# Windowed attention with global rows, then a softplus MLP: global rows through DRAM, a four-slot attention period, and a prologue issued from three queues

## The chip, the core and the metric

The kernel runs on one core of one Trainium2 chip. The metric is the device time of one execution in microseconds (us). The core's engines run side by side, each through its own instruction queue in program order: TensorE (PE in the profile) multiplies matrices into PSUM, VectorE (DVE), ScalarE (ACT) and GpSimd (POOL) work element by element, and SyncE (SP) issues transfers. Transfers can be issued from SP, ACT and POOL; sixteen DMA engines carry them out. Engines wait for one another through semaphores.

## The reference

Eight batches, eight heads, 576 positions, 64 elements per head. Each position attends to the positions within 32 of it and to eight global positions, which are given at run time by `global_idx`; a global position attends to all. The result, as 4608 tokens of 512, goes through a two-layer MLP with softplus.

```python
scores = scale * np.matmul(q, k.transpose(0, 1, 3, 2))
mask = np.abs(pos[:, None] - pos[None, :]) <= window
mask = mask | is_global[:, None] | is_global[None, :]
attn = softmax(np.where(mask, scores, -1e9)); attn_out = np.matmul(attn, v)
x = attn_out.transpose(0, 2, 1, 3).reshape(4608, 512)
h = x @ w_in                                    # 512 -> 2048
out = log(1 + exp(h)) @ w_out                   # 2048 -> 512
```

## The kernel before

**Attention.** A batch is cut into five token tiles (`NTL`), four of 120 positions and one of 96. Behind the positions of each tile stand the eight global rows, so that a tile of 128 (or 104) keys holds its own window and the global keys. The heads are worked on in four pairs `p` (`NP`). Per pair:

- `transposes` (L230) turns five token tiles of K on TensorE into one PSUM tile (`tp`, one buffer) and VectorE copies them to `KT` in two copies (L235, L237); the same again for Q.
- `scores(p, grp)` (L241) multiplies K tiles by the queries in their window: three tiles in group 0 and two in group 1, for both heads. The PSUM tile `sc` has one buffer. ScalarE takes the exponential (L251) and VectorE multiplies by the mask (L252).
- `values(b, h)` (L258), once for each head of the pair, multiplies V (with a block of ones beside it, so that the sums come out as well) by the masked exponentials, into the PSUM tile `av` (one buffer, two banks). VectorE copies sums and values out to `uz` (L278, L279).
- `normalise` (L283) adds up the global rows' parts (L288, L290), makes 1/sum as exp(-ln(sum)) on ScalarE (L292, L293), and GpSimd multiplies (L296, L298) into `xT`, the transposed MLP input.

When a batch's four pairs are done, `globals_out` (L300) writes the eight global rows into their places in `xT` with eight GpSimd copies at positions known at run time (L306).

**Global rows.** SP and POOL read the eight positions into registers (L73). K's and Q's rows of all batches are gathered to `kgf` and `qgf` with eight transfers each (L129), converted and transposed on TensorE once (L216 to L222), and for every batch GpSimd's `glob_cols` (L225 to L228) copies them into the last columns of each tile of `KT` and `QT`. V's rows are gathered into `vg_f` (L134) and put behind each V tile by a small transfer of its own (L111).

**Loading.** Every K, Q and V tile of float32 goes through one ring of six buffers (`ld`, L91). SP issues the load (L93), GpSimd converts to bfloat16 (L98, L115), and a seventh load waits until the oldest conversion is done.

**MLP.** Nine tiles `n` of 512 tokens (`n_tiles`). `mm1(n, s)` (L311) makes 128 hidden rows with four matmuls into `h` (two buffers), and ScalarE makes the softplus from an exponential (L319) and a logarithm (L320). `mm2(n, s)` (L324) does four of the sixteen matmuls of an output block (PSUM tile `o`, one buffer); after the fourth VectorE copies it out (L334) and SP stores it (L335).

**The order.** It is written by hand (`manual_schedule`): what an engine does, and in which sequence, is the order of the calls. First comes a prologue: loads of batch 0, gathers, constants, masks (L138 to L210), the attention of batch 0, and the first slots of batch 1. Then each tile `n` has sixteen slots `s`; a slot calls `mm1(n, s)`, the attention pieces of this slot, and `mm2(n-1, s)`. `attention_slots(b)` (L338) gives batch `b` its slots, counted from the start of tile `b-1`: loads and conversions at -9 to -2, and pair `p` at 3p-3 (transposes), 3p-2 and 3p-1 (scores), 3p+1 and 3p+2 (values), 3p+3 (`normalise`). Tile `n` needs batch `n`, so batch `b` runs beside tile `b-1`; tiles 7 and 8 have no attention beside them.

Of the kernel before, what the change touches and what calls it, by code (L numbers as in the profile page):

```python
# [11 lines left out]
FP32 = mybir.dt.float32  # L12
# [25 lines left out]
def kernel(  # L38
# [22 lines left out]
    nc.scalar.preload_act_table_set("natural_log_exp_and_others")  # L61

# [5 lines left out]
    gidx_i = global_idx.rearrange("(one n) -> one n", one=1).bitcast(I32)  # L68
    idx_i = const.tile([P, 2 * NG], I32)
    nc.sync.dma_start(out=idx_i[:], in_=gidx_i.to_broadcast([P, 2 * NG]))  # L70

    engines = [mybir.EngineType.SP, mybir.EngineType.Pool]
    regs = [  # L73
        nc.values_load(idx_i[0:1, 2 * g:2 * g + 1], engines=engines, min_val=0, max_val=S - 1,
                       skip_runtime_bounds_check_because="positions of the sequence")
        for g in range(NG)
    ]


# [6 lines left out]
    ident = const.tile([P, P], FP32)  # L86
    ident_bf = const.tile([P, P], BF16)


    def load(src, b, t, tag):  # L90
        f = work.tile([P, H, D], FP32, tag="ld", bufs=6, name=f"{tag}_f")  # L91
        s0 = KW * t
        nc.sync.dma_start(out=f[:ST[t]], in_=src[b, :, s0:s0 + ST[t], :].rearrange("h s d -> s h d"))  # L93
        return f

    def load_cast(src, b, t, dst, tag):
        f = load(src, b, t, tag)
        nc.gpsimd.tensor_copy(dst[:ST[t], t], f[:ST[t]].rearrange("p h d -> p (h d)"))  # L98

    def load_k(b):  # L100
        kb = work.tile([P, NTL, d_model], BF16, tag="kb", bufs=1)
        return kb, [lambda t=t: load_cast(k, b, t, kb, "k") for t in range(NTL)]

    def load_q(b):
        qb = work.tile([P, NTL, d_model], BF16, tag="qb", bufs=1)
        return qb, [lambda t=t: load_cast(q, b, t, qb, "q") for t in range(NTL)]

    def load_v_tile(b, t):
        f = load(v, b, t, "v")
        n = ST[t]  # L110
        nc.sync.dma_start(out=f[n:n + NG], in_=vg_f[:, b])  # L111
        dst = V1[b % 2][:, t]
        vf = f[:n + NG].rearrange("p (a e) d -> p a e d", e=2)
        o = dst[:n + NG].rearrange("p a (c d) -> p a c d", d=D)
        nc.gpsimd.tensor_copy(o[:, :, 0:3:2, :], vf)  # L115


    kb0, ks = load_k(0)
    qb0, qs = load_q(0)
    for f in ks:  # L120
        f()

    vg_f = const.tile([NG, B, H, D], FP32)
    kg_f = work.tile([B * NP, NG, 2 * D], FP32, tag="gt", bufs=2, name="kgf")
    qg_f = work.tile([B * NP, NG, 2 * D], FP32, tag="gt", bufs=2, name="qgf")
    for src, dst in ((k, kg_f), (q, qg_f)):
        sv = src.rearrange("b (a e) s d -> (b a) e s d", e=2)
        for g in range(NG):
            nc.sync.dma_start(out=dst[:, g:g + 1, :].rearrange("p o (e d) -> p e o d", e=2),  # L129
                              in_=sv[:, :, bass.ds(regs[g], 1), :])  # L130
    for f in qs:
        f()
    for g in range(NG):
        nc.sync.dma_start(out=vg_f[g:g + 1].rearrange("o b h d -> o (b h) d"),  # L134
                          in_=v.rearrange("b h s d -> (b h) s d")[:, bass.ds(regs[g], 1), :].rearrange("c o d -> o c d"))


    make_identity(nc, ident[:])  # L138
    nc.vector.tensor_copy(ident_bf[:], ident[:])
    for i in range(2):  # L140
        nc.vector.memset(V1[i][:], 0.0)
        nc.vector.memset(V1[i][:, :, :, D:2 * D], 1.0)
    nc.vector.memset(KT[:, :, 4, :], 0.0)
    nc.vector.memset(QT[:, :, 4, :], 0.0)

    idx_f = const.tile([P, NG], FP32)
    nc.vector.tensor_copy(idx_f[:], idx_i[:].rearrange("p (n two) -> p n two", two=2)[:, :, 0])

# [4 lines left out]
    same = work.tile([P, NG, NG], FP32, tag="m1")  # L153
    nc.vector.tensor_tensor(out=same[:], in0=idx_f[:].unsqueeze(2).to_broadcast([P, NG, NG]),
                            in1=idx_f[:].unsqueeze(1).to_broadcast([P, NG, NG]), op=ALU.is_equal)
    nc.vector.tensor_tensor(out=same[:], in0=same[:], in1=low[:], op=ALU.mult)
    uq = work.tile([P, NG], FP32, tag="m2")
    nc.vector.tensor_reduce(out=uq[:], in_=same[:], axis=AX.X, op=ALU.max)
    nc.vector.tensor_scalar(out=uq[:], in0=uq[:], scalar1=-1.0, scalar2=1.0, op0=ALU.mult, op1=ALU.add)
# [3 lines left out]
    kidx = work.tile([P, NTL], FP32, tag="m4")  # L163
    nc.vector.tensor_copy(kidx[:], kidx_i[:])
    keq = work.tile([P, NTL, NG], FP32, tag="m5")
    nc.vector.tensor_tensor(out=keq[:], in0=kidx[:].unsqueeze(2).to_broadcast([P, NTL, NG]),
                            in1=idx_f[:].unsqueeze(1).to_broadcast([P, NTL, NG]), op=ALU.is_equal)
    akey = const.tile([P, NTL], FP32)
    nc.vector.tensor_reduce(out=akey[:], in_=keq[:], axis=AX.X, op=ALU.max)
    nc.vector.tensor_scalar(out=akey[:], in0=akey[:], scalar1=-1.0, scalar2=1.0, op0=ALU.mult, op1=ALU.add)  # L170
    vld = const.tile([P, NTL], FP32)
    nc.gpsimd.memset(vld[:], 1.0)
    ukey = const.tile([P, 2], FP32)
    for i, (s, c) in enumerate(((KW, slice(0, 4)), (ST[4], slice(4, 5)))):
        nc.gpsimd.affine_select(out=vld[:, c], in_=vld[:, c], compare_op=ALU.is_ge, fill=0.0, base=s - 1,
                                channel_multiplier=-1, pattern=[[0, c.stop - c.start]])
        dg = work.tile([P, NG], FP32, tag=f"m6{i}")
        nc.gpsimd.memset(dg[:], 1.0)
        nc.gpsimd.affine_select(out=dg[:], in_=dg[:], compare_op=ALU.is_equal, fill=0.0, base=-s,
                                channel_multiplier=1, pattern=[[-1, NG]])  # L180
        nc.vector.tensor_tensor(out=dg[:], in0=dg[:], in1=uq[:], op=ALU.mult)
        nc.vector.tensor_reduce(out=ukey[:, i:i + 1], in_=dg[:], axis=AX.X, op=ALU.max)
    nc.vector.tensor_tensor(out=akey[:], in0=akey[:], in1=vld[:], op=ALU.mult)
# [11 lines left out]
                            channel_multiplier=1, pattern=[[-1, 32]])  # L195
    masks = [const.tile([P, GW[i]], BF16, name=f"mask{i}") for i in range(2)]
# [16 lines left out]
    gT = []  # L213
    for f in (kg_f, qg_f):
        gb = work.tile([B * NP, NG, 2 * D], BF16, tag="ex0", bufs=2, name="gb")
        nc.vector.tensor_copy(gb[:], f[:])  # L216
        ps = psum.tile([P, NG, B * NP], BF16, tag="tp")
        for g in range(NG):
            nc.tensor.transpose(out=ps[:, g, :], in_=gb[:, g, :], identity=ident_bf[:B * NP, :B * NP])  # L219
        t_ = const.tile([P, B * NP, NG], BF16, name=f"gT{len(gT)}")  # L220
        nc.vector.tensor_copy(t_[:].rearrange("p c g -> p g c"), ps[:])
        gT.append(t_)  # L222


    def glob_cols(b, dst, src):  # L225
        s = src[:, b * NP:(b + 1) * NP, :]
        nc.gpsimd.tensor_copy(dst[:, :, 0:4, KW:KW + NG], s.unsqueeze(2).to_broadcast([P, NP, 4, NG]))  # L227
        nc.gpsimd.tensor_copy(dst[:, :, 4, ST[4]:ST[4] + NG], s)  # L228

    def transposes(src, dst, p):  # L230
        ps = psum.tile([P, NTL * P], BF16, tag="tp", name="tp")
        for t in range(NTL):
            nc.tensor.transpose(out=ps[:, t * P:t * P + ST[t]], in_=src[:ST[t], t, p * P:(p + 1) * P],  # L233
                                identity=ident_bf[:ST[t], :ST[t]])
        nc.vector.tensor_copy(dst[:, p, 0:4, 0:KW],  # L235
                              ps[:, 0:512].rearrange("p (t c) -> p t c", c=P)[:, :, 0:KW])
        nc.vector.tensor_copy(dst[:, p, 4, 0:ST[4]], ps[:, 512:512 + ST[4]])  # L237
# [3 lines left out]
    def scores(p, grp):  # L241
# [9 lines left out]
        nc.scalar.activation(out=ex[:], in_=sc[:, :, 0:GW[grp]], func=ACTF.Exp, scale=SCALE)  # L251
        nc.vector.tensor_tensor(out=ex[:], in0=ex[:], in1=masks[grp][:].unsqueeze(1).to_broadcast([P, 2, GW[grp]]),  # L252
                                op=ALU.mult)
        exps[p, grp] = ex

    UZ = {}

    def values(b, h):  # L258
        p, e = h // 2, h % 2
        av = psum.tile([P, 1024], FP32, tag="av")  # L260
        off = 512 - SPLIT
        parts = []
        for t in range(NTL):
            cuts = [WLO[t]] + ([SPLIT] if WLO[t] < SPLIT < WHI[t] else []) + [WHI[t]]
            for lo, hi in zip(cuts, cuts[1:]):
                parts.append((t, lo, hi))
        for i, (t, lo, hi) in enumerate(parts):
            grp = 0 if t in GRP[0] else 1
            ex = exps[p, grp]
            c = GOFF[t] + lo - WLO[t]  # L270
            nc.tensor.matmul(out=av[:, off + lo:off + hi], lhsT=V1[b % 2][:, t, p, 64 * e:64 * e + 128],  # L271
                             rhs=ex[:, e, c:c + hi - lo],
# [63 lines left out]


    def attention_slots(b):  # L338
        kq = {}

        def loads_kq(which, fs):
            for f in fs:
                f()
# [121 lines left out]
```

## Time and profile before

| | before |
|---|---|
| median of three runs | 505.02 us (504.61 to 507.24) |
| profiled execution, own time | 505.82 us |
| its span, first to last instruction | 504.1 us |
| busy: TensorE, ScalarE, VectorE, GpSimd | 350.6, 272.0, 232.5, 152.9 us |
| transferred by the DMA queues | 43.41 MB |
| mean granted TensorE clock | 0.972 |

Busy times don't add up to the span, since the engines overlap, and a busy TensorE isn't one at full speed: its matmuls are pipelined, and the profile's duration of one includes the pipeline. Spacing between starts is the better measure. In rows of the order of time the columns are start, duration, engine, line, operation, what is written `<-` what is read, the number of instructions merged into the row, and in brackets the idle time before it and what ended it. In rows by group stand the number of instructions, busy time, mean in ns, and idle time of the engine ahead of them.

### The profile page before, as it was taken

What the parts mean: (1) busy time and instruction counts of PE and PEld (TensorE: products, weight loads), DVE (VectorE), ACT (ScalarE), POOL (GpSimd) and SP (SyncE); (2) the same over time, 40 slices, a digit from 0 to 9 for tenths busy, and PEclk for the clock granted to TensorE, in tenths of its full rate; (3) what the DMA queues carried; (4) which work ended last, traced back from release to release, by engine and by line L of the source; (5) the groups of instructions that cost most, each with busy time, mean ns of one, the idle gap of its engine ahead of it and who ended that gap; (6) DMA issues with size and microseconds to landing.
All of it is one profiled execution on the core that took longest, in us unless ns stands there. A gap on an engine that the chain in (4) does not pass through costs nothing.

```text
span 504.1 us, 6355 instructions
## 1 busy us (share of the span) xinstructions
PE 350.6 (70%) x2192; PEld 170.3 (34%) x2192; DVE 232.5 (46%) x479; ACT 272.0 (54%) x417; POOL 152.9 (30%) x310
## 2 busy tenths in 40 slices
PE   0000343102786997799699869968996999999985
PEld 0000222001432443354245425424542544444432
DVE  0028455501584684286358628735862774001111
ACT  1000232201687786488468757856874787766720
POOL 1142311444137135513722461263256113000000
PEclk9999999999987999899899999989998999999999
DMA  5369730099535039425902963391296100111111
GB/s 77 53 114 184 121 58 0 0 169 202 84 59 113 2 82 199 93 61 92 198 23 62 169 127 79 76 198 38 62 169 123 42 22 26 37 42 44 42 43 62
DMA packets 124561, 43.41 MB, mean 86 GB/s; under 512 B 115505, under 2 KB 119601, under 8 KB 124529
## 3 DMA queue, kind: packets, MB, share of 16 engines
q1 hardware_dynamic: 120304, 38.82, 40.9%
q0 software_dynamic: 4224, 4.19, 5.2%
q8 instruction: 17, 0.28, 0.2%
q14 instruction: 16, 0.12, 0.1%
HBM read 37.10 MB, written 9.44 MB: 92 GB/s over the span
## 4 chain that ended last, share of the span: by engine, by line
PE 45%; DMA 18%; ACT 10%; DVE 9%; SPq 6%; issue 6%; POOL 5%; POOLq 0%; DVEq 0%
PE o L330 19%; PE hp L316 17%; DMA v_f<-vg_f 7%; DMA k_f<-in_k_dram 6%; DMA q_f<-in_q_dram 5%; ACT ex L251 4%; PE av L271 4%; PE sc L247 3%; SPq L93 3%; DVE ot L334 2%; ACT e L319 2%; PE tp L233 2%; SPq L129 2%; DVE uz L279 2%; ACT gt L320 2%
## 5 line engine op out<-in xcount | busy, mean ns | idle before, releaser
L330 PE MATMUL o<-w_out_t,gt 128*128 128x512 bf16 x576 | 148.7, 384 | 13.9 <-DVE ot L334 13.9
L316 PE MATMUL hp<-xT,w_in_t 128*128 128x512 bf16 x576 | 155.9, 395 | 0.0
L319 ACT ACTIVATE e<-hp 128x512 f32<-128x512 f32 x144 | 85.6, 595 | 87.5 <-PE hp L316 86.4
L251 ACT ACTIVATE ex<-sc 128x1008 bf16<-128x1008 f32 x64 | 58.3, 912 | 101.0 <-PE sc L247 101.0
L320 ACT ACTIVATE gt<-e 128x512 bf16<-128x512 f32 x144 | 90.9, 632 | 4.6
L296 POOL TENSOR_TENSOR xT<-uz,rz 128x480 bf16<-128x480 f32 x32 | 38.4, 1201 | 174.2 <-ACT rz L293 174.2
L316 PEld LDWEIGHTS <-w_in_t 128*128 128x128 bf16 x576 | 55.8, 101 | 65.3 <-issue 9.3
L330 PEld LDWEIGHTS <-gt 128*128 128x128 bf16 x576 | 51.8, 98 | 73.7 <-issue 24.6
L278 DVE COPY uz<-av 64x616 f32<-64x616 f32 x64 | 51.0, 797 | 37.5 <-PE av L271 36.5
L334 DVE COPY ot<-o 128x512 f32<-128x512 f32 x36 | 24.8, 690 | 71.1 <-PE o L330 70.5
L279 DVE COPY uz<-av 64x616 f32<-64x616 f32 x64 | 51.0, 797 | 1.4
L247 PE MATMUL sc<-QT,KT 64*128 64x200 bf16 (+2 forms) x320 | 26.8, 268 | 23.4 <-POOL QT L227 15.8
L233 PE MATMUL tp<-ident_bf,kb 120*128 120x120 bf16 (+1 forms) x160 | 17.2, 230 | 35.8 <-POOL kb L98 34.4
L252 DVE TENSOR_TENSOR ex<-ex,mask_223 128x1008 bf16<-128x1008 bf16 x32 | 22.2, 693 | 40.4 <-ACT ex L251 39.5
L98 POOL CAST kb<-k_f 120x512 bf16<-120x512 f32 (+1 forms) x40 | 24.6, 615 | 48.7 <-DMA k_f<-in_k_dram 48.7
L219 PE MATMUL ps<-ident_bf,gb 32*128 32x32 bf16 x16 | 0.8, 185 | 51.2 <-DVE gb L216 51.2
L98 POOL CAST qb<-q_f 120x512 bf16<-120x512 f32 (+1 forms) x40 | 27.1, 678 | 26.1 <-DMA q_f<-in_q_dram 26.1
L235 DVE COPY KT<-tp 128x480 bf16<-128x480 bf16 x32 | 13.0, 406 | 40.2 <-PE tp L233 40.0
L292 ACT ACTIVATE rz<-uz 128x616 f32<-128x616 f32 x32 | 22.5, 704 | 16.2 <-DVE uz L278 16.2
L271 PE MATMUL av<-ex,V_0_106 128*128 128x160 bf16 (+2 forms) x192 | 20.8, 253 | 10.5 <-DVE uz L279 10.4
L233 PEld LDWEIGHTS <-kb 120*128 120x128 bf16 (+1 forms) x160 | 12.8, 105 | 45.3 <-POOL kb L98 36.9
L252 DVE TENSOR_TENSOR ex<-ex,mask_224 128x800 bf16<-128x800 bf16 x32 | 18.4, 576 | 20.5 <-ACT ex L251 19.9
(76 smaller groups left out, 245.4 us busy)
## 6 DMA issues: line engine op xcount, KB each, us to landing
out_dram<-ot SPq DMA_DIRECT2D x36, 256.0 KB
k_f<-in_k_dram SPq DMA_DIRECT2D x32, 240.0 KB
q_f<-in_q_dram SPq DMA_DIRECT2D x32, 240.0 KB
v_f<-in_v_dram SPq DMA_DIRECT2D x32, 240.0 KB
w_in_t<-in_moe_w_in_dram POOLq DMA_DIRECT2D x4, 512.0 KB, 8.1
w_out_t<-in_moe_w_out_dram POOLq DMA_DIRECT2D x4, 512.0 KB, 9.6
k_f<-in_k_dram SPq DMA_DIRECT2D x8, 192.0 KB
q_f<-in_q_dram SPq DMA_DIRECT2D x8, 192.0 KB
```

The costliest lines, as they stand in the source:

```text
L98: nc.gpsimd.tensor_copy(dst[:ST[t], t], f[:ST[t]].rearrange("p h d -> p (h d)"))
L233: nc.tensor.transpose(out=ps[:, t * P:t * P + ST[t]], in_=src[:ST[t], t, p * P:(p + 1) * P], identity=ident_bf[:ST[t], :ST[t]])
L247: nc.tensor.matmul(out=sc[:, e, GOFF[t]:GOFF[t] + w], lhsT=KT[r, p, t, :], rhs=QT[r, p].rearrange("p t c -> p (t c)")[:, WLO[t]:WHI[t]], s ...
L251: nc.scalar.activation(out=ex[:], in_=sc[:, :, 0:GW[grp]], func=ACTF.Exp, scale=SCALE)
L252: nc.vector.tensor_tensor(out=ex[:], in0=ex[:], in1=masks[grp][:].unsqueeze(1).to_broadcast([P, 2, GW[grp]]), op=ALU.mult)
L271: nc.tensor.matmul(out=av[:, off + lo:off + hi], lhsT=V1[b % 2][:, t, p, 64 * e:64 * e + 128], rhs=ex[:, e, c:c + hi - lo], start=(lo in ( ...
L278: nc.vector.tensor_copy(UZ[p][ur, 1, :], av[zr, off:off + NPOS])
L279: nc.vector.tensor_copy(UZ[p][ur, 0, :], av[ur, off:off + NPOS])
L316: nc.tensor.matmul(out=hp[:], lhsT=w_in_t[:, kd, kf * P:(kf + 1) * P], rhs=xT[:, kd, n * NT:(n + 1) * NT], start=(kd == 0), stop=(kd == KD ...
L319: nc.scalar.activation(out=e[:], in_=hp[:], func=ACTF.Exp)
L320: nc.scalar.activation(out=gts[n][:, kf, :], in_=e[:], func=ACTF.Ln, bias=1.0)
L330: nc.tensor.matmul(out=op[:], lhsT=gts[n][:, kf, i * P:(i + 1) * P], rhs=w_out_t[:, kf, :], start=(kf == 0), stop=(kf == KF - 1))
```

## The change

**Global rows.** Three DRAM buffers hold the eight rows of all batches for K, Q and V. Each is gathered once, with eight transfers; K's and V's are issued from ScalarE, Q's from GpSimd, and the positions are read into registers of those two. For each batch and tensor two transfers on SP then put the rows behind the five token tiles in a float32 tile that holds the whole batch. There is one such tile each for K, Q and V, in place of the ring. A conversion takes all 128 partitions of a token tile, rows included, and so K and Q are transposed together with their global rows, 128 columns a tile, and copied out with one copy. The separate transposing of the rows, `glob_cols` and the zeroing of `KT`, `QT` and V's tiles are gone; the unused partitions of the last tile are zeroed in the float32 tile.

**Period.** Pair `p` starts at slot 4p-6 and is spread over the two halves of the slots: half 0 stands between `mm1` and `mm2`, half 1 behind `mm2`. Loads are issued at slots -18 (K), -15 (Q) and -11 (V), conversions stand at -9 to -4. `normalise` is split into the sums of the global rows, logarithm, exponential and scaling, at slots of their own.

**Prologue.** SP issues the loads of K and Q of batch 0 first, then V, then the rows; the index is loaded from ScalarE. VectorE converts K and GpSimd converts Q and V of batch 0. In batch 0's attention ScalarE copies Q's transposes and the sums, Q's transposes use a buffer of `h`, and the value products stand between the other pieces. The loads of `w_out` move into the first four slots of tile 0.

```diff
+    stage = {n: const.tile([P, NTL, d_model], FP32, name=f"{n}_f") for n in "kqv"}
+    grow = {n: nc.dram_tensor(f"{n}_global_rows", (NG, B * H * D), FP32, kind="Internal").ap() for n in "kqv"}
+    def load(n, b, eng=None):
+        eng = eng or nc.sync
+        for t in range(NTL):
+            s0 = KW * t
+            eng.dma_start(out=stage[n][:ST[t], t].rearrange("p (h d) -> p h d", d=D),
+                          in_=src[n][b, :, s0:s0 + ST[t], :].rearrange("h s d -> s h d"))
+    def load_rows(n, b, eng=None):
+        eng = eng or nc.sync
+        g = grow[n][:, b * H * D:(b + 1) * H * D]
+        eng.dma_start(out=stage[n][KW:P, 0:4], in_=g.unsqueeze(1).to_broadcast([NG, 4, H * D]))
+        eng.dma_start(out=stage[n][ST[4]:ST[4] + NG, 4], in_=g)
+    def gather(n, eng, regs):
+        sv = src[n].rearrange("b h s d -> (b h) s d")
         for g in range(NG):
+            eng.dma_start(out=grow[n][g:g + 1].rearrange("o (c d) -> c o d", d=D),
+                          in_=sv[:, bass.ds(regs[g], 1), :])
+    def cast_tile(n, b, t, eng):
+        if n == "v":
+            o = V1[b % 2][:, t].rearrange("p a (c d) -> p a c d", d=D)[:, :, 0:3:2, :]
+            eng.tensor_copy(o, stage[n][:, t].rearrange("p (a e d) -> p a e d", e=2, d=D))
+            return
+        if t == 0:
+            kqb[n] = work.tile([P, NTL, d_model], BF16, tag=f"{n}b", bufs=1, name=f"{n}b")
+        eng.tensor_copy(kqb[n][:, t], stage[n][:, t])
...
+    for n in "kqv":
+        nc.gpsimd.memset(stage[n][96:P, 4], 0.0)
+    load("k", 0)
+    load("q", 0)
...
+    gather("k", nc.scalar, regs)
+    gather("q", nc.gpsimd, regs)
+    gather("v", nc.scalar, regs)
+    load("v", 0)
+    for n in "kqv":
+        load_rows(n, 0)
...
-    def glob_cols(b, dst, src):
...
+    def transposes(n, p, tag="tp", copy=None):
+        dst = KT if n == "k" else QT
+        ps = psum.tile([P, 2 * 512], BF16, tag=tag, bufs=2 if tag == "h" else 1, name="tp")
         for t in range(NTL):
+            nc.tensor.transpose(out=ps[:, t * P:(t + 1) * P], in_=kqb[n][:, t, p * P:(p + 1) * P],
+                                identity=ident_bf[:])
+        (copy or nc.vector.tensor_copy)(dst[:, p].rearrange("p t c -> p (t c)"), ps[:, 0:NTL * P])
...
-        nc.vector.tensor_copy(UZ[p][ur, 1, :], av[zr, off:off + NPOS])
+        (zcopy or nc.vector.tensor_copy)(UZ[p][ur, 1, :], av[zr, off:off + NPOS])
...
+        at(-18, 1, load, "k", b)
+        at(-18, 1, load_rows, "k", b)
+        at(-15, 1, load, "q", b)
+        at(-15, 1, load_rows, "q", b)
+        at(-11, 1, load, "v", b)
+        at(-11, 1, load_rows, "v", b)
         for t in range(NTL):
+            at(-9 + t // 3, 0, cast_tile, "k", b, t, nc.gpsimd)
+            at(-8 + t // 3, 1, cast_tile, "q", b, t, nc.gpsimd)
+            at(-6 + t // 2, 1, cast_tile, "v", b, t, nc.gpsimd)
         for p in range(NP):
+            s = 4 * p - 6
+            at(s, 0, transposes, "k", p)
+            at(s, 1, transposes, "q", p)
+            at(s + 1, 0, scores, p, 0)
+            at(s + 1, 1, mask, p, 0)
+            at(s + 2, 0, scores, p, 1)
+            at(s + 2, 1, mask, p, 1)
+            at(s + 3, 0, values, b, p, 0)
+            at(s + 4, 1, values, b, p, 1)
+            at(s + 5, 1, glob_sums, b, p)
+            late = 1 if p < NP - 1 else 0
+            at(s + 6 + late, 0, inv_ln, p)
+            at(s + 6 + 2 * late, 0, inv_exp, p)
+            at(s + 6 + 2 * late, 1, scale_x, b, p)
+        at(12, 1, glob_norm, b)
+        at(12, 1, glob_out, b)
...
+    act_copy = lambda o, i: nc.scalar.copy(out=o, in_=i)
     for t in range(NTL):
+        cast_tile("k", 0, t, nc.vector)
+    for t in range(NTL):
+        cast_tile("q", 0, t, nc.gpsimd)
     CW = 512
...
+    for t in range(NTL):
+        cast_tile("v", 0, t, nc.gpsimd)
...
     for p in range(NP):
+        transposes("k", p)
+        transposes("q", p, "h", act_copy)
+        if p:
+            values(0, p - 1, 0, act_copy)
         scores(p, 0)
+        mask(p, 0)
+        if p:
+            values(0, p - 1, 1, act_copy)
         scores(p, 1)
+        mask(p, 1)
+        if p:
+            glob_sums(0, p - 1)
+            inv_ln(p - 1)
+            inv_exp(p - 1)
+            scale_x(0, p - 1)
...
     for n in range(n_tiles + 1):
         for s in range(16):
             if n < n_tiles:
                 mm1(n, s)
+            for b in (n + 1, n + 2, n + 3):
+                attend(b, s - 16 * (b - n - 1), 0)
+            if n == 0 and s < 4:
+                nc.gpsimd.dma_start(out=w_out_t[:, 4 * s:4 * s + 4, :],
+                                    in_=moe_w_out[4 * s * P:(4 * s + 4) * P, :].rearrange("(a p) f -> p a f", p=P))
             if n > 0:
                 mm2(n - 1, s)
+            for b in (n + 1, n + 2, n + 3):
+                attend(b, s - 16 * (b - n - 1), 1)
```

More of the change, by code (lines that the diff above doesn't have):

```diff
@@ L100, in load_k @@
[L100 to L115, printed above, removed]
@@ L131 @@
[L131 to L135, printed above, removed]
+    src = {"k": k, "q": q, "v": v}
+    grow = {n: nc.dram_tensor(f"{n}_global_rows", (NG, B * H * D), FP32, kind="Internal").ap() for n in "kqv"}
[5 more added lines that the diff above has]
+                          in_=src[n][b, :, s0:s0 + ST[t], :].rearrange("h s d -> s h d"))
@@ new lines @@
+    kqb = {}
+    def cast_tile(n, b, t, eng):
[6 more added lines that the diff above has]
+        eng.tensor_copy(kqb[n][:, t], stage[n][:, t])
+    nc.scalar.dma_start(out=idx_i[:], in_=global_idx.rearrange("(one n) -> one n", one=1).bitcast(I32)
+                        .to_broadcast([P, 2 * NG]))
@@ L386, with attend @@
                             in_=moe_w_in[:, c * CW:(c + 1) * CW].rearrange("(a p) f -> p a f", p=P))
+    for t in range(NTL):
+        cast_tile("v", 0, t, nc.gpsimd)
+    att = {b: attention_slots(b) for b in range(1, B)}
+    done = set()
+    def attend(b, s, half):
+        for f, a in att.get(b, {}).get((s, half), []):
+            f(*a)
+        att.get(b, {}).pop((s, half), None)
+    for s in range(-18, -9):
+        attend(1, s, 0)
+        attend(1, s, 1)
     for p in range(NP):
-        transposes(kb0, KT, p)
@@ L389 @@
-        transposes(qb0, QT, p)
+        transposes("k", p)
+        transposes("q", p, "h", act_copy)
+        if p:
+            values(0, p - 1, 0, act_copy)
         scores(p, 0)
+        mask(p, 0)
+        if p:
+            values(0, p - 1, 1, act_copy)
         scores(p, 1)
-        if p > 0:
-            values(0, 2 * p - 2)
-            values(0, 2 * p - 1)
-            normalise(0, p - 1)
-    values(0, 6)
-    values(0, 7)
-    normalise(0, 3)
-    globals_out(0)
-    for c in range(4):
-        nc.gpsimd.dma_start(out=w_out_t[:, 4 * c:4 * c + 4, :],
-                            in_=moe_w_out[4 * c * P:(4 * c + 4) * P, :].rearrange("(a p) f -> p a f", p=P))
@@ L420 @@
+    values(0, 3, 0, act_copy)
+    values(0, 3, 1, act_copy)
+    glob_sums(0, 3)
+    inv_ln(3)
+    inv_exp(3)
+    scale_x(0, 3)
+    glob_norm(0)
+    glob_out(0)
     for s in range(-9, 0):
-        for f in att[1].get(s, []):
-            if f is not None:
-                f()
+        for half in range(2):
+            attend(1, s, half)
+            attend(2, s - 16, half)
     for n in range(n_tiles + 1):
         for s in range(16):
-            pre, post = attention_at(n, s) if n < n_tiles else ([], [])
@@ L438 @@
+    assert not any(att.values())
 _INS = ['q', 'k', 'v', 'global_idx', 'moe_w_in', 'moe_w_out']
```

204 lines of the change are left out of this document (62 added, 142 removed).

## The prediction

> **What bounds the kernel now.** I read the page first, then busy time per stretch, then the order of time at the seams, then TensorE's order inside a stage, and last the durations by group. The page's chain of waits says that no single engine holds the end: TensorE has less than half of it, transfers nearly a fifth.
>
> ```profile
> PE 45%; DMA 18%; ACT 10%; DVE 9%; SPq 6%; issue 6%; POOL 5%; POOLq 0%; DVEq 0%
> q0 software_dynamic: 4224, 4.19, 5.2%
> ```
>
> So I cut the span where the first `mm1` of the tiles 0, 1, 6 and 7 starts. The columns are stretch, length, busy time of TensorE, of its weight loads, VectorE, ScalarE and GpSimd, the granted clock, the share of the DMA engines and GB/s.
>
> ```profile
> 0.00:53.30 53.30, 0.78 (x16) 0.67 (x17) 16.14 (x43) 1.28 (x1) 13.12 (x39) 1.00 0.64 103
> 53.30:99.60 46.30, 16.57 (x128) 10.57 (x127) 25.11 (x50) 13.13 (x16) 11.38 (x22) 1.00 0.29 46
> 99.60:124.90 25.30, 3.12 (x21) 1.61 (x22) 1.53 (x5) 1.01 (x1) 12.04 (x22) 1.00 1.11 176
> 124.90:164.60 39.70, 30.56 (x195) 14.42 (x194) 24.59 (x51) 30.26 (x47) 16.60 (x34) 0.88 0.49 87
> 164.60:388.80 224.20, 193.45 (x1282) 94.13 (x1281) 131.55 (x269) 156.54 (x242) 91.91 (x178) 0.96 0.56 104
> 388.80:426.60 37.80, 35.67 (x237) 17.75 (x236) 24.58 (x49) 29.83 (x48) 7.83 (x16) 1.00 0.08 28
> ```
>
> A quarter of the span, 124.9 us, passes before the first `mm1`: 53 us of loading and set-up in which TensorE does almost nothing, 46 us of attention for batch 0 alone, and 25 us in which TensorE waits for the loads of batch 1. The five stages of tiles 1 to 5 then take 224.2 us, 44.8 each, and TensorE is busy in 86% of them. The order of time shows why the prologue is long:
>
> ```profile
> 0.82 0.39 SPq L70 DMA_DIRECT2D idx_i<-in_global_idx_dram  x1
> 6.13 4.34 SPq L93 DMA_DIRECT2D k_f<-in_k_dram  x5
> 9.81 0.61 POOL L98 CAST kb<-k_f 120x512 bf16<-120x512 f32 x1 [9.29 <-DMA k_f<-in_k_dram]
> 10.68 6.22 SPq L129 DMA_DIRECT2D kgf<-in_k_dram  x8
> 22.91 4.57 SPq L93 DMA_DIRECT2D q_f<-in_q_dram  x5
> 53.35 0.64 PE L233 MATMUL tp<-ident_bf,kb 120*128 120x120 bf16 x5 [1.38 <-DVE gT_267 L221]
> ...
> 97.52 2.05 POOL L306 COPY xT<-xg 128x4 bf16 x8
> 103.36 0.33 SPq L93 DMA_DIRECT2D k_f<-in_k_dram  x1
> 103.39 0.28 PE L233 MATMUL tp<-ident_bf,kb 120*128 120x120 bf16 x1 [9.95 <-POOL kb L98]
> 124.88 1.89 PE L316 MATMUL hp<-xT,w_in_t 128*128 128x512 bf16 x4
> ```
>
> SP issues everything, one after another: nothing until the index has come and been read (6.13), then K, sixteen gathers, and Q only at 22.9. Attention starts at 53.35. At 103 the loads of batch 1 go on only as GpSimd's casts free the six buffers.
>
> **The change, prologue.** SP issues K, Q and V of batch 0 from 0.8 us on, and waits for no index. That is 3 x 576 x 512 x 4 bytes = 3.54 MB, at the 176 GB/s of the third stretch 20.1 us, and 3.7 us from issue to first landing (6.13 to 9.81): V ends near 24.6. The gathers take 6.22 us for eight issues; K's and V's go one after the other on ScalarE from about 6.1, Q's beside them on GpSimd, so all are issued by 18.5. Their landing in DRAM isn't in this trace; between 2 and 6 us more they stay hidden behind the V load. The row loads stand behind V on SP and its queue, so K's rows land at 25.5 and Q's at 26.5 (24 if they slip past V, 35 if each of the six costs 1.7 us in line). That is the step that now gates attention, because a cast reads the whole tile with its rows. What goes away there (transposing the rows on TensorE, `glob_cols`, the zeroing of `KT`, `QT` and `V1`) ran off this path or just ahead of 53.35 and costs nothing more.
>
> ```profile
> L319 ACT ACTIVATE e<-hp 128x512 f32<-128x512 f32 x144 | 85.6, 595 | 87.5 <-PE hp L316 86.4
> L320 ACT ACTIVATE gt<-e 128x512 bf16<-128x512 f32 x144 | 90.9, 632 | 4.6
> L278 DVE COPY uz<-av 64x616 f32<-64x616 f32 x64 | 51.0, 797 | 37.5 <-PE av L271 36.5
> L296 POOL TENSOR_TENSOR xT<-uz,rz 128x480 bf16<-128x480 f32 x32 | 38.4, 1201 | 174.2 <-ACT rz L293 174.2
> L251 ACT ACTIVATE ex<-sc 128x1008 bf16<-128x1008 f32 x32 | 32.0, 1000 | 98.0 <-PE sc L247 97.9
> L251 ACT ACTIVATE ex<-sc 128x800 bf16<-128x800 f32 x32 | 26.3, 823 | 3.0 <-PE sc L247 3.0
> L293 ACT ACTIVATE rz<-rz 128x616 f32<-128x616 f32 x32 | 23.0, 718 | 1.0
> L98 POOL CAST kb<-k_f 120x512 bf16<-120x512 f32 x32 | 19.7, 616 | 46.5 <-DMA k_f<-in_k_dram 46.5
> L252 DVE TENSOR_TENSOR ex<-ex,mask_224 128x800 bf16<-128x800 bf16 x32 | 18.4, 576 | 20.5 <-ACT ex L251 19.9
> L235 DVE COPY KT<-tp 128x480 bf16<-128x480 bf16 x32 | 13.0, 406 | 40.2 <-PE tp L233 40.0
> L237 DVE COPY KT<-tp 128x96 bf16<-128x96 bf16 x32 | 6.3, 198 | 0.0
> ```
>
> Q's five casts on GpSimd end at 26.5 + 5 x 0.62 = 29.6, K's on VectorE run beside them. A transpose group (0.64), its copy on ScalarE (a PSUM copy there isn't in the trace: 0.6 to 0.8, by the 0.72 of the 616-column activation; I take 0.65) and the two scores with their exponentials end the first head pair at 34. Each further round is set by ScalarE: Q copy 0.65, two sum copies 0.7, exponentials 1.00 and 0.82, logarithm and exponential 0.72 each, together 5.3 us; before, 46.3 us for four pairs is 11.6 a round. The first of the three has no normalisation yet (3.9) but waits about 1 us for V's casts, which stand on GpSimd behind Q's casts and the issues of `w_in`. So: 39, 44.3, 49.6; the tail of the last pair (mask, two value products with their copies, logarithm, exponential) about 6, GpSimd's scaling 1.6 and the eight row copies 2.05: **59**.
>
> Ahead of the first `mm1` now stand batch 1's whole first head pair and the second's transposes and first scores. On GpSimd the casts follow the row copies: ten casts, 6.2 us, to 65.4. Then a bare chain, with nothing to hide it: transposes 0.6, copy 0.5, scores 0.6, exponential 1.0, scores 0.5, exponential 0.8, mask 0.6, values 0.95, two copies 1.6, values 0.95, two copies 1.6, copy 0.5, scores 0.4 = 10.6 us. First `mm1` at **76** instead of 124.9. The transfers allow it: two batches at 20 us, and `w_in` at 13 (both weights took 5.2% of 504.1 us), with 4 us at the start make 57. Bounds: 64 (rows early, GpSimd's casts overlapped) and 92 (rows at 35, 176 GB/s not held beside `w_in`).
>
> **The change, stages.** TensorE's order is written out, and warm it costs this much:
>
> ```profile
> 400.50 0.56 PE L271 MATMUL av<-ex,V_1_107 128*128 128x160 bf16 x6
> 400.99 0.39 PE L247 MATMUL sc<-QT,KT 64*128 64x160 bf16 x6
> 401.31 1.04 PE L330 MATMUL o<-w_out_t,gt 128*128 128x512 bf16 x4
> 402.19 1.03 PE L316 MATMUL hp<-xT,w_in_t 128*128 128x512 bf16 x4
> 403.05 0.56 PE L271 MATMUL av<-ex,V_1_107 128*128 128x160 bf16 x6
> 403.54 0.34 PE L247 MATMUL sc<-QT,KT 64*128 64x200 bf16 x4
> 403.81 1.04 PE L330 MATMUL o<-w_out_t,gt 128*128 128x512 bf16 x4
> 405.55 0.42 PE L233 MATMUL tp<-ident_bf,kb 120*128 120x120 bf16 x5
> 405.81 1.03 PE L330 MATMUL o<-w_out_t,gt 128*128 128x512 bf16 x4
> ...
> 408.01 0.56 PE L271 MATMUL av<-ex,V_1_107 128*128 128x160 bf16 x6
> ```
>
> From start to start: values 0.49, scores 0.32 and 0.27, `mm1` and `mm2` 0.86, a transpose group 0.26. One head pair in three slots takes 7.51 us (400.50 to 408.01), nearly dense, so a stage of twelve such slots and four bare ones (1.73) would be 36.9; the 7.9 us above that are the waits for casts and loads at the batch seam. The change takes those away: loads are issued 9, 7 and 5 slots ahead of their casts, and 20 us of transfer fit into a stage.
>
> But the four-slot period has waits of its own. Call its slots A (both transposes, and the second value product of the pair before), B and C (scores), D (first value product). Dense it is 8 x 0.86 + 2 x 0.26 + 0.32 + 0.27 + 2 x 0.49 = 9.0 us. In A, VectorE's queue has the two 0.80 copies of the value product ahead of the Q copy. From the end of the value product: 0.2 until the copies start, 1.6, then the Q copy of 640 columns (between 0.41 and 0.60; 0.49 by the slope between 96 and 480) and 0.06 make 2.3, while TensorE has only a transpose group and one `mm1`, 1.1. **Wait in B: 1.2 us.** In C, ScalarE takes `e` and `gt` of that slot's `mm1` (1.2) ahead of the second exponential (0.82), then comes the mask (0.58): with 0.3 of hand-overs 2.9 us from the end of that `mm1`, while TensorE has scores, `mm2`, `mm1` and the first two value matmuls, 2.15. **Wait in D: 0.75 us.** The period is 10.95, four of them 43.8; at slot 12 the last pair's logarithm and exponential stand in front of the next batch's exponential and add 1.4: **45.2 a stage**, against 44.8. ScalarE has 8.2 us in a period and doesn't bind. So the waits at the seam are spread over the stage rather than won.
>
> In the first stage there is no `mm2`; the same chains make a period of 9.25, so 38.4 against 39.7. In tile 6 eleven slots keep attention: two and a half such periods and five bare slots, 37.7 against 37.8. Tiles 7, 8 and the end don't change.
>
> **Sum.** 504.1 - (124.9 - 76) - 1.3 + 5 x 0.4 - 0.1 = 455.8 us of span. The profiled execution took 505.82 us, 1.7 beside its span and 0.8 above the median of the runs shown: 457.5, or **457 us** beside the median.
>
> **Rivals.** First, the two waits are covered, by copies that finish sooner or by value matmuls that run ahead of the mask: then a stage is 36 to 37.5, six stages gain about 7 each: **416**. For it: the three-slot rows are within 0.25 us of dense. Against: the same lines wait behind each other in program order there too, only with a slot more between.
>
> Second, the prologue stays with the transfers: the rows land at 35, and batch 1's V and `w_in` share the queues, so that the first `mm1` comes at 92 to 95: **476**. The third stretch speaks for it, where the DMA share is 1.11 at only 176 GB/s. Near it, the change doesn't do what it says: casts wait for the last gather through POOL's queue and the first `mm1` stays above 105, **487** or more.
>
> Third, slower: the short waits keep TensorE at half clock.
>
> ```profile
> 384.58 1.89 PE L330 MATMUL o<-w_out_t,gt 128*128 128x512 bf16 x4
> ```
>
> After a seam a group of four takes 1.89 and not 1.03. If two waits in each period held it there, a bare slot would be 3.4 and a stage about 68, so 457 + 5 x 23 = **572**; slower begins when a stage passes 55 us, at some 40% of its time at half clock. Against: at 0.86 busy the stages have a clock of 0.96, and in tile 6, where a seam is absent, 1.00.
>
> The Trainium skill, TensorE: Matmul & The Clock Gate, A second HAM failure mode: psum-queue depth-cycling, speaks for this rival: frequent micro-idles between groups make the clock swing. The same page, HAM oscillation — how this bites in real kernels, puts the limit at gaps of about 3.4 us; by that rule waits of 1.2 us change nothing and the sum stands. The trace so far agrees with the second.
>
> **How the numbers follow.** The forecast has 0.55, covered waits 0.20, transfers 0.15, a change that does little 0.05, the half clock 0.05. The range reaches down to most of the covered-waits case and up to the transfers case: **420 to 476 us**. A measurement here tells about 0.5% from no change. Faster 0.93, the same 0.02, slower 0.05.
>
> **What would show it.** In the profile after: first transposes near 30, the row copies of batch 0 ending near 59, the first `mm1` near 76. In tiles 1 to 5: stages near 45, two waits of TensorE per period, one for the Q copy by VectorE and one for the mask, and no cast waiting for a transfer. It is wrong if stages are near 37, if the first attention waits for rows long after 27, or if the granted clock falls below 0.9 there.

## The result, and the profile after

The changed kernel takes 489.9 us (median; 489.05 to 490.5) against 506.1 for the kernel before: a ratio of 0.967, interval 0.961 to 0.973. It is faster, by 3% and not by the 10% of the forecast, and outside its range. The profiled execution took 490.01 us with a span of 488.4 us.

First the busy time per stretch in the changed kernel, cut as in the prediction (start of the first `mm1` of tiles 0, 1, 6 and 7) and once more at 27.2 and 63.6; columns as there.

```profile
0.00:27.20 27.20, 0.02 (x1) 0.03 (x1) 8.22 (x37) 1.28 (x1) 8.96 (x33) 1.00 0.90 154
27.20:63.60 36.40, 18.59 (x128) 10.95 (x128) 17.96 (x34) 20.67 (x28) 17.45 (x30) 1.00 0.96 162
63.60:80.40 16.80, 7.65 (x49) 4.47 (x51) 6.67 (x12) 2.16 (x3) 10.61 (x19) 1.00 1.09 171
80.40:122.30 41.90, 27.67 (x189) 14.20 (x191) 24.70 (x42) 30.77 (x48) 18.02 (x32) 0.92 0.85 133
122.30:373.20 250.90, 195.57 (x1257) 97.88 (x1281) 134.73 (x227) 157.89 (x241) 86.37 (x155) 0.94 0.47 86
373.20:410.90 37.70, 33.66 (x205) 16.50 (x208) 19.97 (x37) 28.67 (x46) 7.82 (x16) 1.00 0.08 29
```

| stretch | before | after | forecast |
|---|---|---|---|
| up to the first `mm1` | 124.9 | 80.4 | 76 |
| tile 0 | 39.7 | 41.9 | 38.4 |
| tiles 1 to 5 | 224.2 | 250.9 | 226 |
| tile 6 | 37.8 | 37.7 | 37.7 |
| rest | 77.5 | 77.5 | 77.5 |

The prologue gave 44.5 us, nearly all that was expected, and tiles 0 to 5 took 29 of them back. A stage is 50.2 us (250.9 / 5) and not 45.2. The order of time shows the prologue first:

```profile
16.02 4.94 SPq L83 DMA_DIRECT2D v_f<-in_v_dram  x5
21.09 0.35 SPq L89 DMA_DIRECT2D k_f<-k_global_rows  x1
26.69 2.18 DVE L107 CAST kb<-k_f 128x512 bf16<-128x512 f32 x5 [15.00 <-DMA k_f<-k_global_rows]
...
33.46 15.97 SPq L83 DMA_DIRECT2D q_f<-in_q_dram  x5
...
61.64 2.04 POOL L299 COPY xT<-xg 128x4 bf16 x8
63.61 2.82 POOL L107 CAST kb<-k_f 128x512 bf16<-128x512 f32 x5
```

The rows are issued at 21 behind V's load and gate the first conversion at 26.7; GpSimd converts batch 1's K only behind the row copies of batch 0. Then TensorE's order in one period, from slot A's `mm1` to the next A, left out are only groups that waited for no other engine:

```profile
179.68 1.03 PE L309 MATMUL hp<-xT,w_in_t 128*128 128x512 bf16 x4
181.80 0.40 PE L227 MATMUL sc<-QT,KT 64*128 64x160 bf16 x6 [1.10 <-DVE QT L217]
...
186.71 0.40 PE L252 MATMUL av<-ex,V_1_73 128*128 128x72 bf16 x4 [0.41 <-DVE ex L236]
...
190.49 1.03 PE L309 MATMUL hp<-xT,w_in_t 128*128 128x512 bf16 x3
```

The period is 10.81 us, with the two waits at the two places that were forecast. What was not forecast stands at slot 13, where the next batch's first value product comes. TensorE, then ScalarE and GpSimd ahead of it:

```profile
157.93 0.32 PE L252 MATMUL av<-ex,V_1_73 128*128 128x160 bf16 x2
160.39 0.43 PE L252 MATMUL av<-ex,V_1_73 128*128 128x72 bf16 x3 [2.14 <-DVE ex L236]
163.29 0.30 PE L252 MATMUL av<-ex,V_1_73 128*128 128x144 bf16 x1 [2.47 <-POOL V_1_73 L103]
...
165.09 1.91 PE L309 MATMUL hp<-xT,w_in_t 128*128 128x512 bf16 x4
```

```profile
157.19 0.70 ACT L275 ACTIVATE rz<-uz 128x616 f32<-128x616 f32 x1
157.92 0.72 ACT L278 ACTIVATE rz<-rz 128x616 f32<-128x616 f32 x1
158.54 0.82 ACT L231 ACTIVATE ex<-sc 128x800 bf16<-128x800 f32 x1
```

```profile
158.71 1.20 POOL L284 TENSOR_TENSOR xT<-uz,rz 128x480 bf16<-128x480 f32 x1 [2.97 <-ACT rz L278]
159.87 0.72 POOL L286 TENSOR_TENSOR xT<-uz,rz 128x96 bf16<-128x96 f32 x1
160.66 2.05 POOL L299 COPY xT<-xg 128x4 bf16 x8
162.63 0.61 POOL L103 CAST V_1_73<-v_f 128x512 bf16<-128x512 f32 x1
```

The product waits twice. First 2.14 us for the mask, because the last pair's logarithm and exponential stand ahead of its exponential on ScalarE. Then 2.47 us for V's fifth token tile: in slot 12 the old batch's scaling and row copies are called first, and the new batch's fifth conversion stands behind both on GpSimd. From there on TensorE is at half clock (1.91 for a group of four `mm1`, 1.03 otherwise); the clock granted reads 1.00 up to 160, 0.75 from 160 to 161 and 0.50 from 161 to 167.

### The profile page after: what moved, and what is told of

Its sections match the earlier page's. It is cut to its first block, busy times and chain, and to the rows that moved or that the text cites. A ratio compares the mean times of both kernels' runs of the same rounds, so it can differ in the third digit from the quotient of the medians.

```text
span 488.4 us, 6167 instructions
## 1 busy us (share of the span) xinstructions
PE 353.2 (72%) x2136; PEld 175.1 (36%) x2176; DVE 221.0 (45%) x400; ACT 280.8 (58%) x429; POOL 149.2 (31%) x284
## 3 DMA queue, kind: packets, MB, share of 16 engines
q1 hardware_dynamic: 118944, 39.73, 43.4%
## 4 chain that ended last, share of the span: by engine, by line
PE 30%; issue 24%; POOL 22%; ACT 9%; DVE 6%; DMA 5%; SPq 2%; POOLq 1%; ACTq 0%; DVEq 0%
PE o L323 15%; PE hp L309 11%; POOL qb L107 5%; POOL kb L107 4%; POOL xT L284 4%; PE av L252 3%; ACT ex L231 2%; POOL V_0_72 L103 2%; DVE uz L260 2%; POOL xT L299 2%; DMA v_f<-v_global_rows 2%; ACT e L312 2%; ACT gt L313 2%; DMA q_f<-in_q_dram 2%; POOL V_1_73 L103 2%
## 5 line engine op out<-in xcount | busy, mean ns | idle before, releaser
L309 PE MATMUL hp<-xT,w_in_t 128*128 128x512 bf16 x561 | 153.0, 393 | 1.4 <-issue 0.5
L284 POOL TENSOR_TENSOR xT<-uz,rz 128x480 bf16<-128x480 f32 x32 | 38.4, 1200 | 238.9 <-ACT rz L278 238.9
L259 DVE COPY uz<-av 64x616 f32<-64x616 f32 x56 | 44.6, 797 | 54.8 <-PE av L252 51.4
L260 DVE COPY uz<-av 64x616 f32<-64x616 f32 x64 | 51.0, 797 | 10.9 <-ACT uz L367 9.7
L215 PE MATMUL tp<-ident_bf,kb 128*128 128x128 bf16 x160 | 18.7, 249 | 35.4 <-DVE kb L107 27.6
L252 PE MATMUL av<-ex,V_0_72 128*128 128x160 bf16 (+2 forms) x192 | 24.9, 255 | 26.1 <-DVE ex L236 11.9
L252 PE MATMUL av<-ex,V_1_73 128*128 128x160 bf16 (+2 forms) x192 | 22.4, 240 | 24.6 <-DVE ex L236 13.9
L236 DVE TENSOR_TENSOR ex<-ex,mask_212 128x800 bf16<-128x800 bf16 x32 | 22.0, 687 | 37.1 <-ACT ex L231 36.9
L227 PEld LDWEIGHTS <-KT 64*128 64x128 bf16 x320 | 13.4, 98 | 60.3 <-issue 56.3
L107 POOL CAST qb<-q_f 128x512 bf16<-128x512 f32 x40 | 27.5, 729 | 14.1 <-DMA v_f<-v_global_rows 14.1
L236 DVE TENSOR_TENSOR ex<-ex,mask_211 128x1008 bf16<-128x1008 bf16 x32 | 24.9, 779 | 12.4 <-ACT ex L231 12.4
L215 PEld LDWEIGHTS <-kb 128*128 128x128 bf16 x160 | 13.7, 112 | 45.9 <-DVE kb L107 28.5
L252 PEld LDWEIGHTS <-V_0_72 128*128 128x128 bf16 x192 | 16.3, 107 | 37.3 <-issue 21.5
L252 PEld LDWEIGHTS <-V_1_73 128*128 128x128 bf16 x192 | 14.8, 102 | 35.9 <-issue 17.7
```

What stands on the lines that cost most here:

```text
L107: eng.tensor_copy(kqb[n][:, t], stage[n][:, t])
L227: nc.tensor.matmul(out=sc[:, e, GOFF[t]:GOFF[t] + w], lhsT=KT[r, p, t, :], rhs=QT[r, p].rearrange("p t c -> p (t c)")[:, WLO[t]:WHI[t]], s ...
L259: (zcopy or nc.vector.tensor_copy)(UZ[p][ur, 1, :], av[zr, off:off + NPOS])
L260: nc.vector.tensor_copy(UZ[p][ur, 0, :], av[ur, off:off + NPOS])
L284: nc.gpsimd.tensor_tensor(out=x[:, 0:480].rearrange("p (t c) -> p t c", c=KW), in0=a(uz[:, 0]), in1=a(rz[:]), op=ALU.mult)
L309: nc.tensor.matmul(out=hp[:], lhsT=w_in_t[:, kd, kf * P:(kf + 1) * P], rhs=xT[:, kd, n * NT:(n + 1) * NT], start=(kd == 0), stop=(kd == KD ...
```

## The experiments

Each ratio is to the kernel before, run beside it; the intervals are 0.004 to 0.0075 to each side. Between the groups of runs the median of the kernel before itself went from 506.1 to 508.6 us, so a difference of under 3 us between two of these kernels says nothing. The changed kernel's 489.9 us is the mark for e1 to e7.

**V's conversions a slot earlier (e1).** Nothing of the new batch's V is then behind the row copies.

```diff
-            at(-6 + t // 2, 1, cast_tile, "v", b, t, nc.gpsimd)
+            at(-6 + t // 3, 1, cast_tile, "v", b, t, nc.gpsimd)
```

> The changed kernel with the last two conversions of V one slot earlier (slot -5), so that none stands behind the eight row copies of the batch before on GpSimd. Theory G (GpSimd's queue at the seam): the second wait at slot 13 of each stage (2.4 us, for V's last conversion) and the half-clock groups after it go, six times 3 to 3.5 us: 468 to 472 us; the first wait there, for the mask (2.1 us), stays. Theory S (ScalarE's logarithm and exponential ahead of the next exponential make the seam): the mask comes as late as before, V's conversion is hidden behind it, gain under 5 us, 485 us or more. Theory D (rows or loads of V land late): V's conversion now waits for a transfer, no gain, 488 us or more.

466.2 us (ratio 0.918), a little under the 468 to 472 expected. One line gives 24 us. The same place in this kernel, and then its tiles 1 to 5:

```profile
155.70 0.32 PE L252 MATMUL av<-ex,V 128*128 128x160 bf16 x2
158.16 0.40 PE L252 MATMUL av<-ex,V 128*128 128x72 bf16 x4 [2.14 <-DVE ex L236]
```

```profile
119.40:349.10 229.70, 187.39 (x1259) 95.32 (x1281) 134.99 (x227) 158.40 (x243) 86.29 (x155) 0.99 0.51 94
```

Tiles 1 to 5 now take 229.7 us, 45.9 a stage: the forecast's 45.2 was that of a kernel without this place in GpSimd's queue. The 2.14 us are still there, the second wait is gone, and the clock in the stages is 0.99 and not 0.94. No load or row transfer is what V waits for: behind the prologue, GpSimd waits for no transfer in this trace.

**Logarithm and exponential behind the next exponential (e2).** Only for a batch's last pair.

```diff
-            at(s + 6 + late, 0, inv_ln, p)
-            at(s + 6 + 2 * late, 0, inv_exp, p)
+            at(s + 6 + late, 0 if late else 1, inv_ln, p)
+            at(s + 6 + 2 * late, 0 if late else 1, inv_exp, p)
```

> The changed kernel with the logarithm and the exponential of a batch's last pair moved behind mm2 in slot 12, so that ScalarE takes the next batch's exponential first. Theory G: the mask is ready 1.4 us sooner, but V's last conversion still stands behind scaling and row copies, and these start 0.8 us later: no gain, 489 to 496 us. Theory S: the seam loses its wait of 2.1 us and more, six times 2 to 4 us: 466 to 478 us.

495.0 us (0.974), 5 us above the changed kernel and within what theory G expects. From seam to seam its trace has 51.1 us, where the changed kernel has 50.2. The mask does come sooner, but all that GpSimd has queued comes later:

```profile
159.75 0.33 PE L252 MATMUL av<-ex,V 128*128 128x72 bf16 x3 [0.42 <-DVE ex L236]
164.75 0.30 PE L252 MATMUL av<-ex,V 128*128 128x144 bf16 x1 [4.67 <-POOL V L103]
```

Of the two waits the later one decides, and removing the earlier alone gains nothing; it lost about 1 us a stage.

**Both (e3).**

> Both edits together. Theory G with S as its second half: waits at slot 13 shrink to the 0.4 to 0.7 us that the other periods have for the mask, and the seam stays at full clock: stages of 43.5 to 44.5 us, 490 - 6 x 5.5 = 457 us, 453 to 462. If something else holds the seam (a transfer, the half clock by itself), 470 us or more.

450.8 us (0.888), a little under the expected range. Tiles 1 to 5:

```profile
116.40:333.50 217.10, 183.99 (x1257) 94.08 (x1281) 133.30 (x227) 157.69 (x241) 84.86 (x155) 1.00 0.54 100
```

A stage is 43.4 us, four periods of 10.85 with nothing at the seam, at a clock of 1.00. So the seam cost 39 us, more than twice what e1 and e2 add up to (24 - 5): the second edit is worth 15 us once the first is made.

**The three-slot period in the changed kernel (e7).** Early loads, rows through DRAM and prologue stay.

```diff
-            s = 4 * p - 6
+            s = 3 * p - 3
...
-            at(s + 3, 0, values, b, p, 0)
-            at(s + 4, 1, values, b, p, 1)
+            at(s + 4, 0, values, b, p, 0)
+            at(s + 5, 0, values, b, p, 1)
...
+            at(s + 6, 0, inv_ln, p)
+            at(s + 6, 0, inv_exp, p)
+            at(s + 6, 0, scale_x, b, p)
```

> The changed kernel with the three-slot period of the kernel before in place of the four-slot one (order of the pieces in a slot as there); rows through DRAM, early loads and the prologue stay. Theory P (the four-slot order itself makes the waits in every period, the early loads remove the seam): stages of 37 to 39 us against 49.9, first mm1 between 70 and 80: 420 to 432 us. Rival (early loads and rows hold the stages wherever the pieces stand): stages of 44 or more, 455 us or more.

420.4 us (0.828), within the range; the stages are a little above the 37 to 39 us expected. Tiles 1 to 5, and then a wait of TensorE over the whole kernel, in the kernel before and in this one:

```profile
108.60:307.20 198.60, 186.41 (x1275) 95.47 (x1299) 135.76 (x233) 158.14 (x245) 85.36 (x156) 1.00 0.60 110
```

```profile
PE o L330 <- DVE ot L334: 13.9, 21, 0.9
```

```profile
PE o L323 <- DVE ot L327: 13.4, 21, 0.8
```

Stages of 39.7 us, against 44.8 in the kernel before with the same period: the early loads and the rows in the token tile, which no run takes apart, do remove the waits for loads and conversions at the seam, as the prediction said. The waits that stay are those of `mm2` for the copy of its own output, about 2 us a stage in both kernels; the prediction counted them among the 7.9 us at the seam. The four-slot order alone, as it was written, costs 70 us of what the rest of the change gives. The 39 us of its seam are among them, since in e7 the row copies are called in slot 13, behind V's last conversion.

**Q's copy on ScalarE (e4) and the first value product behind `mm2` (e5).** Each takes away the cause of one of the two waits in a period; both on the changed kernel.

```diff
-            at(s, 1, transposes, "q", p)
+            at(s, 1, transposes, "q", p, "tp", act_copy)
```

> The changed kernel with the copy of Q's transposes on ScalarE in the stages too, so that it doesn't stand behind the two 0.80 copies of the value product on VectorE. Theory P: the wait of 1.1 us in slot B, 28 times, goes, the seam stays: 490 - 28 = 462 us, 458 to 468. Rival (ScalarE, 0.69 more in each period, takes the wait over: the mask of slot D comes later by it): less than half of that is won, 475 us or more.

```diff
-            at(s + 3, 0, values, b, p, 0)
+            at(s + 3, 1, values, b, p, 0)
```

> The changed kernel with the first value product of a pair behind mm2 in its slot and not ahead of it, 0.86 us later on TensorE. Theory P: the waits for the mask in slot D (0.2 to 0.65 us, some 24 of them, about 12 us) go, and at the seam 0.9 of the 4.5 us is covered each time (5 us): 470 to 476 us. Rival (the wait moves on to the second value product, which now finds the PSUM tile taken): 484 us or more.

462.2 us (0.911) and 472.6 us (0.931), both as expected. Waits of TensorE in total, times and longest, first of the changed kernel, then with Q's copy on ScalarE, then with the value product later:

```profile
PE sc L227 <- DVE QT L217: 30.8, 28, 1.7
PE av L252 <- DVE ex L236: 25.8, 31, 2.8
```

```profile
PE av L252 <- DVE ex L236: 23.2, 31, 2.7
```

```profile
PE av L252 <- DVE ex L236: 13.0, 13, 2.8
```

With Q's copy on ScalarE the wait of the scores for VectorE's copy is no longer in the list at all, and the mask hasn't become later by ScalarE's extra 0.69 us. With the product later, 31 waits for the mask become 13.

**All four edits (e6).**

> The four-slot period with all four edits (V's conversions earlier, logarithm and exponential behind the next exponential, Q's copy on ScalarE, first value product behind mm2). Theory P: no wait of the period or the seam is left, stages of 37 to 38.5 us, 415 to 425 us. Rival (ScalarE, with 8.9 us of 9.2 in a period, becomes the bound): stages of 40 us or more, 430 us or more.

413.5 us (0.816), just under the range.

```profile
114.60:300.10 185.50, 183.05 (x1282) 93.56 (x1282) 125.41 (x210) 168.09 (x263) 87.19 (x155) 1.00 0.63 116
```

A stage is 37.1 us and TensorE is busy in 99% of it: the four-slot period is then nearly as dense as its matmuls (four times 9.0 is 36). ScalarE at 168 of 185.5 doesn't bind.

**The prologue (e9, e11, e12).** e9 is the three-slot kernel e7 with the rows of K and Q ahead of V's load, e11 is e6 with the same, and e12 adds batch 1's conversions of K and Q ahead of the last pair's value products in the order of the calls (the second part of the edit).

```diff
-    load("v", 0)
-    for n in "kqv":
-        load_rows(n, 0)
+    load_rows("k", 0)
+    load_rows("q", 0)
+    load("v", 0)
+    load_rows("v", 0)
...
+    for s in (-9, -8, -7):
+        for half in range(2):
+            attend(1, s, half)
+            attend(2, s - 16, half)
     values(0, 3, 0, act_copy)
     values(0, 3, 1, act_copy)
```

> The kernel with early loads and the three-slot period (420.4 us), with the rows of K and Q issued ahead of the load of V of batch 0. If the rows' place behind V sets the start of attention, as the prediction has it: first transposes near 19 and not 26.4, first mm1 5 to 7 us sooner, 413 to 416 us. If the gathers' landing or V's conversion sets it, the start moves by less than 2 us: 418 to 421 us.

414.8 us (0.819), 5.6 less than e7. The first transposes come at 19.6 and not 26.4, and the first `mm1` 4.7 us sooner (66.8, in e7 71.5), a little less than expected. The rows are issued ahead of V's load, and the conversion starts at 19.1, in e7 at 25.9:

```profile
16.60 0.28 SPq L89 DMA_DIRECT2D k_f<-k_global_rows  x1
19.11 1.77 DVE L107 CAST kb<-k_f 128x512 bf16<-128x512 f32 x5 [7.42 <-DMA k_f<-k_global_rows]
```

> The four-slot kernel with all four edits (413.5 us) and the rows of K and Q ahead of V's first load. If the start of attention sets the first mm1 in this kernel as in the three-slot one, where the edit was worth 5.7 us: 407 to 409 us. If something in the prologue takes it back: 412 us or more.

408.6 us (0.806), as expected.

> The same, and GpSimd converts K and Q of batch 1 ahead of the scaling of batch 0's last pair, not behind its row copies. If GpSimd's queue sets the end of the prologue, as the prediction has it (ten conversions of 0.56 to 0.62 us behind the row copies): the chain of batch 1 starts up to 6 us sooner, 402 to 406 us. If the loads of batch 1, which share the DMA engines with w_in, are what is late: no more than 1 us gained, or a loss, 407 us or more.

403.9 us (0.796, interval 0.789 to 0.803), as expected and the fastest of all. GpSimd's queue in it:

```profile
50.59 2.84 POOL L107 CAST kb<-k_f 128x512 bf16<-128x512 f32 x5
53.51 2.84 POOL L107 CAST qb<-q_f 128x512 bf16<-128x512 f32 x5
56.32 1.20 POOL L285 TENSOR_TENSOR xT<-uz,rz 128x480 bf16<-128x480 f32 x1
57.47 0.39 POOL L287 TENSOR_TENSOR xT<-uz,rz 128x96 bf16<-128x96 f32 x1
57.92 2.51 POOL L300 COPY xT<-xg 128x4 bf16 x8
```

The conversions run in the time in which GpSimd waited, K and Q of batch 1 are there at 56, and the row copies end at 60.4. So the queues on SP and GpSimd set the length of the prologue, as the prediction's working had it, and there was still 10 us to be had by order alone.

## Why the prediction was wrong

**What bounds the kernel, and the prologue: right, 4.4 us too short.** Rows behind V were put at 25.5 and gated the conversion at 26.7. From the end of the row copies to the first `mm1` 17 us were worked out and 16.8 measured, in part by luck: the conversions took 5.6 us and not 6.2, the chain behind them 11.2 and not 10.6. The first pair ended at 35.2 and not 34, V's conversions delayed the first round by more than the 1 us assumed, and the later rounds were under-sized, 5.3 against 6.0 us; with these the row copies end at 63.6 and not 59. The 0.7 us of a round can be read in the changed kernel:

```profile
43.93 0.67 ACT L367 COPY uz<-av 64x616 f32<-64x616 f32 x1
...
44.63 0.79 DVE L260 COPY uz<-av 64x616 f32<-64x616 f32 x1 [1.15 <-ACT uz L367]
...
45.48 0.91 PE L252 MATMUL av<-ex,V_0_72 128*128 128x160 bf16 x6 [0.91 <-DVE uz L260]
...
46.42 0.67 ACT L367 COPY uz<-av 64x616 f32<-64x616 f32 x1 [0.79 <-PE av L252]
```

The working let the two copies of a value product run beside each other on two engines; VectorE's starts only after ScalarE's, the second product waits for it, and ScalarE then stands idle for 0.79 us.

**The period: right.** 10.95 was worked out and 10.81 to 11.04 measured away from the seam, with 1.10 for the Q copy (forecast 1.2) and 0.41 to 0.65 for the mask (forecast 0.75). Experiments e4 to e6 remove these waits by their causes. Tile 6 came out at the 37.7 us forecast by luck: two and a half periods and five bare slots, the terms given for it, make 36.0.

**The seam: wrong, and this is the step that failed.** The step "at slot 12 the last pair's logarithm and exponential stand in front of the next batch's exponential and add 1.4" looked at ScalarE's queue only. The mask wait came as described, 2.14 us in place of the period's 0.4 to 0.65. But the same slot was not followed through GpSimd's queue, where scaling, eight row copies and the next batch's last V conversion stand in line. The slot numbers were in the diff (the conversion at -6 + 4 // 2, slot 12 of the tile; `glob_out` at 12) and the durations in the rows quoted (1.20, 2.05, 0.62). Nor was the half clock behind a long wait given a price. With both, the seam added 50.2 - 43.4 = 6.8 us and not 1.4; e1 takes away GpSimd's part with most of the half clock, 50.2 - 45.9 = 4.3 us, and e3 the rest. A stage is 5.0 us above the forecast, 25 us over five stages, and tile 0, where the same seam stands, another 3.5. With the prologue's 4.4 the forecast of the span then becomes 455.8 + 4.4 + 3.5 + 25 = 488.7, measured 488.4; that this closes is no proof, since the differences are those of the measured stretches. The proof is e1, which mends GpSimd's queue alone and has nearly the forecast's stages, and e3, where nothing is left of the seam.

**The rivals.** The covered waits (416) were not what this change does, but all four edits come near that price: 413.5. The transfers didn't hold the prologue: the six row transfers of batch 0 were issued within 3 us (21.09 to 24.0), so that nothing like the bound of 35 came about. For batch 1 they didn't either, although Q's second load took 16 us to issue (33.46) beside `w_in`: GpSimd came to its conversions only at 63.6. The half clock as a consequence of the short waits in the period fell: at 1.10 and up to 0.65 us in each of them e3 has 1.00 in its stages. The Trainium skill (TensorE: Matmul & The Clock Gate, HAM oscillation — how this bites in real kernels) puts the limit at idle gaps of about 3.4 us. e3 agrees with that, but the seams don't. In the seam shown above the clock falls between 160 and 161, where the first wait of 2.14 us has just ended. In e1, which has this wait alone, it still falls at two of the five seams (0.52 from 205 to 208, 0.50 from 297 to 300). This could be read before the change: the group of 1.89 that the prediction quotes for this rival stands behind a wait of 2.68 us, so that "the trace so far agrees" with the limit was a wrong reading. The row just ahead of it in the kernel before:

```profile
384.04 0.60 PE L247 MATMUL sc<-QT,KT 64*128 64x160 bf16 x6 [2.68 <-POOL QT L227]
```

**The range** held the known waits' bounds from both sides, but took the queue at the seam as known, and so its upper end stood on the prologue alone.

## What to carry to other kernels

When a schedule is written by hand, follow each slot through every engine's queue, not only through the one whose chain is being priced: at the place where two batches meet, list for each engine what the old one calls ahead of the new one. A slot that calls the old batch first puts the end of its work in front of the start of the next, and a conversion that takes 0.6 us can then hold TensorE for 2.5 us, and in e2 for 4.7. Where an instruction group waits twice, mend the later wait first; mending the earlier one alone gained nothing here.

## What the hardware showed that was not expected

The granted clock that the profile shows isn't to be trusted in the prologue, where it reads 1.00 until it first falls. In the changed kernel the prologue reads 1.00 from 27.2 to 63.6, yet a value product of six matmuls takes there what it takes in a stretch of e3 that reads 0.51, and not the 0.56 of the warm stages. First the changed kernel, then e3's stretch, then its product:

```profile
56.85 0.91 PE L252 MATMUL av<-ex,V_0_72 128*128 128x160 bf16 x6 [1.66 <-DVE uz L260]
...
189.81 0.56 PE L252 MATMUL av<-ex,V_1_73 128*128 128x160 bf16 x6
```

```profile
46.00:84.00 38.00, 17.74 (x109) 9.54 (x107) 16.95 (x32) 15.74 (x22) 16.75 (x32) 0.51 1.03 160
```

```profile
50.92 0.91 PE L252 MATMUL av<-ex,V 128*128 128x160 bf16 x6 [0.92 <-DVE uz L260]
```

Two runs of e6, of 413.34 and 412.72 us, read 0.996 and 0.962 in the mean, so that the mean over a whole kernel doesn't rank kernels either.

And the time to issue depends on what is under way: five loads that SP issued in 4.94 us at 16.02 took it 15.97 us at 33.46, after GpSimd had issued `w_in`, and 8.56 us at 6.17, ahead of `w_in`. That the DMA queue was full is not shown; no run took `w_in` away.
